# Layer norm of the first tile alone at the front: rstd by ACT, no bias operation, two warm matmuls fewer

## The chip, the cores and the metric

The kernel runs on one core of a Trainium2 chip. The metric is the device time of one execution in microseconds (us). PE is TensorE, DVE VectorE, ACT ScalarE, POOL GpSimd; SP issues the DMAs. PEclk is the granted clock of PE as a share of full speed. All runs below gave correct results, and all count as "fast" by the state rule; the differences are under 1%, so most kernels were timed five or six times, beside runs of the kernel before on the same chip.

## The reference

Four residual blocks over x of 2048 tokens by 512 features, in bf16: attention, feed-forward, attention, feed-forward, each behind a layer norm.

```
x = x + A(layernorm(x), wqkv, wo)     # linear attention, 32 heads of 16
x = x + B(layernorm(x), w1, w2)       # relu feed-forward, 1376 hidden
... the same two again
layernorm(x) = (x - mean(x)) / sqrt(var(x) + 1e-5)
A: q, k, v = x @ wqkv;  phi(t) = where(t > 0, t + 1, exp(t)) + 1e-6
   o = phi(q) (phi(k)^T v) / (phi(q) . sum phi(k));  A = o @ wo
```

## The kernel before

The 2048 tokens are 16 tiles of 128. The kernel is a list of operations with the buffers that they read and write; a list scheduler written in Python orders them for each engine, with a table of durations, a model of the DMA loads, and a seeded random search (1200 tries) that keeps an order when its modelled score, nearly the total time, is no worse. The order per engine is then fixed: an engine takes its instructions one by one, in program order, each behind waits on semaphores. This is why a small change of the operations gives another order of everything.

What matters here is the head, the first 25 us. The loads are issued in this order: x tile 0, x tiles 1-3, the K weights (wk), x tiles 4-7, the Q weights, more x. For tiles 0-3 each tile has its own layer norm and is transposed by PE; tiles 4-15 go in fours, and their transposes are DMAs of two tiles.

```
# cut: the layer norm of one of the tiles 0-3, before
if i in ACT_STATS:                       # tiles 2 and 3: sum and sum of squares by ACT
    ACT  activation(sqscr, xin[i], Identity, accum_out=s1)      # sm
    ACT  activation(sqscr, xin[i], Square,   accum_out=s2)      # sq
    DVE  mean, nm2, var                                          # three tiny operations
else:                                    # tiles 0 and 1
    DVE  bn_stats, bn_aggr
DVE  veps  = max(var, 0) + eps
POOL rstd  = veps ** -0.5
DVE  nbias = -mean * rstd
DVE or ACT  xn = xin * rstd + nbias      # norm
PE   4 transposes 128x128 into PSUM ; ACT or DVE copies them to Tb ; PE projects k (kproj)
# cut: warm-up, before any data is there
for k in range(12):  PE matmul of zeros, 128x512
# cut: the scheduler's model of a load: done = max(start + 1600, dma_free) + xfer_ns + 500
# cut: the choice in the scheduler: among operations that can start within 150 ns (DVE) of the
#      earliest one, the one of highest priority; priority of tile i is raised by 3000 * (16 - i)
```

## Time and profile before

Three runs at first, median 289.81 us (289.64 to 290.19); in later rounds single executions lie between 289.3 and 290.7, medians between 289.9 and 290.0.

The first part of the page, kernel before: busy time of each engine, its share of the span and its number of instructions.

```profile
PE 282.3 (98%) x1447; PEld 127.9 (44%) x1447; DVE 175.3 (61%) x482; ACT 177.7 (62%) x362; POOL 35.0 (12%) x45
```

PE is busy nearly all the time, but this counts 4.9 us of warm matmuls that compute nothing. The waits of PE, kernel before (who waited for whom, total, times, longest):

```profile
PE ps L563 <- DVE wrm L556: 1.2, 1, 1.2
PE ps L672 <- ACT Tb L642: 0.9, 2, 0.7
PE ps L672 <- DVE big L852: 0.5, 1, 0.5
PE ps L638 <- DVE xn L614: 0.4, 1, 0.4
PE ps L672 <- DMA Tb<-xn: 0.2, 1, 0.2
```

Only the wait on `big L852` (near 131 us) lies outside the head. The timeline of the head, kernel before, cut to the norms and to PE (start, duration, engine, line, operation, then in brackets the idle time ahead and what ended it):

```profile
3.69 0.18 DVE L583 BATCH_NORM_AGGREGATE mv<-bst 128x2 f32<-128x6 f32 x1
...
4.15 0.58 POOL L925 TENSOR_TENSOR rstd<-veps,nhalf 128x1 f32<-128x1 f32 x1 [1.72 <-DVE veps L923]
...
5.03 0.41 DVE L614 TENSOR_SCALAR xn<-xin,rstd,nbias 128x512 bf16<-128x512 bf16 x1
...
6.70 0.41 DVE L614 TENSOR_SCALAR xn<-xin,rstd,nbias 128x512 bf16<-128x512 bf16 x1
...
7.03 1.04 PE L672 MATMUL ps<-wqkv,Tb 128*128 128x512 bf16 x4 [0.69 <-ACT Tb L642]
...
8.52 1.29 DVE L582 BATCH_NORM_STATS2 bst<-xin 128x6 f32<-128x512 bf16 x2 [0.56 <-DMA xin<-in_A_x_dram]
...
8.98 1.04 PE L672 MATMUL ps<-wqkv,Tb 128*128 128x512 bf16 x4 [0.24 <-ACT Tb L642]
```

Tile 0's norm starts 1.16 us after its aggregate ended (3.87). The k projections of tiles 0 and 1 (kproj0, kproj1) start at 7.03 and 8.98. The chain that ended last, kernel before, in order of time (start, duration, what):

```profile
2.23 6.26 DMA xin<-in_A_x_dram
...
8.52 1.29 DVE bst L582 x2
...
19.60 5.17 DMA Tb<-xn
...
24.82 105.58 PE ps L672 x572
```

The chain does not run through PE's head, but through the load of x tiles 4-7, DVE, and the DMA transpose of tiles 8-9, which is used by kproj8 at 24.82. Two paths, PE's and DVE's, reach that point almost together.

### The profile page before, as it was taken

Reading aid. Unit: us, or ns where it says so; the run is one execution under the profiler, and the core shown is the slowest. Engines: PE = TensorE matmul, PEld = TensorE weight load, DVE = VectorE, ACT = ScalarE, POOL = GpSimd, SP = SyncE. Lnnn points to the kernel's source line nnn. Section 1 sums busy time; section 2 is a strip of 40 time slices with the busy share of each in tenths; the row PEclk is TensorE's granted clock in tenths of the full one; section 3 lists DMA queues with packets and bytes.
Section 4 is the critical chain, followed back from the end, with each engine's and each line's share of the span. In section 5 each row is a group of like instructions: output and inputs, shape, how many; then the busy total and the mean of one; then the engine's idle time right before and its main releaser. Section 6 shows DMA issues by size and latency. Waiting matters only on the chain.

```text
span 288.4 us, 3983 instructions
## 1 busy us (share of the span) xinstructions
PE 282.3 (98%) x1447; PEld 127.9 (44%) x1447; DVE 175.3 (61%) x482; ACT 177.7 (62%) x362; POOL 35.0 (12%) x45
## 2 busy tenths in 40 slices
PE   7999999999999999999999999999999999999996
PEld 2444454444444444443444444444444444444444
DVE  5899539998358652493345786899854954130233
ACT  5997649999666483586533665999966427316000
POOL 4211000002001110050301373000110011000000
PEclk9999999999999999999999999999999999999999
DMA  7976760213003070030003120012300323001022
GB/s 225 349 101 93 218 211 0 54 22 73 0 2 73 0 146 2 1 73 0 3 0 73 34 41 0 0 35 40 75 2 0 73 71 77 0 32 43 0 73 73
DMA packets 40163, 17.22 MB, mean 60 GB/s; under 512 B 31985, under 2 KB 39633, under 8 KB 40145
## 3 DMA queue, kind: packets, MB, share of 16 engines
q1 hardware_dynamic: 40144, 16.98, 24.8%
q8 instruction: 11, 0.18, 0.3%
q14 instruction: 8, 0.06, 0.1%
HBM read 7.01 MB, written 2.10 MB: 32 GB/s over the span
## 4 chain that ended last, share of the span: by engine, by line
PE 90%; DVE 4%; DMA 4%; SPq 0%; issue 0%; ACT 0%
PE ps L672 90%; DMA xin<-in_A_x_dram 2%; DMA Tb<-xn 2%; DVE bst L582 2%; DVE xn L614 1%; DVE big L658 0%; DVE emscr L656 0%; DVE big L852 0%; DVE mv L583 0%; ACT big L851 0%; DVE xin L870 0%; SPq L539 0%; SPq L534 0%; SPq L536 0%; DVE veps L590 0%
## 5 line engine op out<-in xcount | busy, mean ns | idle before, releaser
L672 PE MATMUL ps<-Tb,w 128*128 128x512 bf16 (+1 forms) x352 | 78.5, 379 | 0.5 <-DVE big L852 0.5
L672 PE MATMUL ps<-w,big 128*128 128x512 bf16 (+2 forms) x363 | 77.3, 372 | 0.0
L851 ACT ACTIVATE big<-ps 128x512 bf16<-128x512 f32 (+1 forms) x79 | 47.0, 601 | 28.2 <-PE ps L672 27.8
L679 ACT ACTIVATE sqscr<-xres 128x512 bf16<-128x512 f32 x48 | 30.0, 626 | 39.3 <-DVE xres L716 25.9
L672 PEld LDWEIGHTS ps<-w,big 128*128 128x128 bf16 (+1 forms) x363 | 35.5, 98 | 40.8
L672 PEld LDWEIGHTS ps<-Tb,w 128*128 128x128 bf16 (+1 forms) x352 | 34.5, 100 | 41.6 <-issue 1.8
L654 ACT ACTIVATE escr<-ps 128x512 bf16<-128x512 f32 x64 | 37.8, 617 | 8.4 <-PE ps L672 8.2
L652 ACT ACTIVATE big<-ps 128x512 bf16<-128x512 f32 x64 | 38.5, 619 | 2.5 <-PE ps L672 2.5
L712 DVE SCALAR_TENSOR_TENSOR xin<-ps,rstdf,xres 128x512 bf16<-128x512 f32 x15 | 11.3, 750 | 37.6 <-PE ps L672 37.5
L672 PE MATMUL ps<-wqkv,Tb 128*128 128x512 bf16 x128 | 31.9, 379 | 1.2 <-ACT Tb L642 0.9
L672 PE MATMUL ps<-big,xn 128*128 128x512 bf16 x128 | 32.2, 379 | 0.0
L658 DVE TENSOR_TENSOR big<-big,emscr 128x512 bf16<-128x512 bf16 x64 | 30.0, 484 | 3.4 <-ACT big L652 2.1
L656 DVE TENSOR_SCALAR emscr<-escr 128x512 bf16<-128x512 bf16 x64 | 21.2, 342 | 14.6 <-ACT escr L654 14.0
L672 PE MATMUL ps<-Tb,wqkv 128*128 128x512 bf16 x128 | 30.0, 379 | 0.0
L672 PE MATMUL ps<-Wp,big 128*128 128x512 bf16 x128 | 29.3, 379 | 0.0
L716 DVE SCALAR_TENSOR_TENSOR xres<-ps,rstdf,xres 128x512 f32<-128x512 f32 x16 | 12.0, 750 | 22.3 <-PE ps L672 22.1
L705 POOL TENSOR_TENSOR rstdf<-varf,nhalf 128x4 f32<-128x4 f32 x8 | 8.3, 1042 | 132.7 <-DVE nm2f L699 75.2
L830 DVE TENSOR_TENSOR big<-big,ps 128x512 bf16<-128x512 bf16 x32 | 20.0, 681 | 3.4 <-PE ps L672 3.4
L672 PEld LDWEIGHTS ps<-wqkv,Tb 128*128 128x128 bf16 x128 | 12.1, 98 | 16.2 <-ACT Tb L642 1.6
L672 PEld LDWEIGHTS ps<-Wp,big 128*128 128x128 bf16 x128 | 12.2, 98 | 15.4 <-DVE Wp L762 0.8
L672 PEld LDWEIGHTS ps<-Tb,wqkv 128*128 128x128 bf16 x128 | 12.2, 98 | 15.0 <-DVE nmf L688 0.5
L672 PEld LDWEIGHTS ps<-big,xn 128*128 128x128 bf16 x128 | 12.2, 98 | 14.6 <-issue 0.5
(89 smaller groups left out, 201.4 us busy)
## 6 DMA issues: line engine op xcount, KB each, us to landing
wqkv<-in_A_wqkv_dram SPq DMA_DIRECT2D x3, 512.0 KB, 7.2
xin<-in_A_x_dram SPq DMA_DIRECT2D x3, 512.0 KB, 8.2
out_dram<-xin SPq DMA_DIRECT2D x3, 512.0 KB, 2.9
w<-in_B_w_dram SPq DMA_DIRECT2D x1, 1376.0 KB, 6.5
w<-in_B_w_dram SPq DMA_DIRECT2D x1, 1280.0 KB, 9.6
wo<-in_A_wo_dram SPq DMA_DIRECT2D x1, 512.0 KB, 8.8
Tb<-xn SPq DMA_TRANSPOSE x30, 3.2
xin<-in_A_x_dram SPq DMA_DIRECT2D x1, 384.0 KB, 3.0
```

Of the source, the lines that this page charges most:

```text
L582: g.add(DVE, lambda e: e.bn_stats(bst[:, i, :], xin[:, i, :]), [("xin", i)], [("bst", i)], C_DVE_BNST, name="bnst%d" % i)
L652: g.add(ACT, lambda e: e.activation(dst_ap, psv[:, b, :], ACTF.Identity, bias=1.0 + 1e-6, scale=1.0), [("ps", b)], [dst_key], C_ACT_PSUM, ...
L654: g.add(ACT, lambda e: e.activation(escr[:, s, :], psv[:, b, :], ACTF.Exp), [("ps", b)], [("escr", s)], C_ACT_EXP, name=name + "_exp")
L656: g.add(DVE, lambda e: e.tensor_scalar(emscr[:, s, :], escr[:, s, :], 1.0, 1e-6, ALU.min, ALU.add), [("escr", s)], [("emscr", s)], C_DVE_B ...
L658: g.add(DVE, lambda e: e.tensor_tensor(dst_ap, dst_ap, emscr[:, s, :], ALU.max), [dst_key, ("emscr", s)], [dst_key], 340.0, name=name + "_ ...
L672: last = e.matmul(o, l, r, start=st, stop=sp, skip_group_check=skip)
L679: g.add(ACT, lambda e: e.activation(sqscr[:, q, :], xres[:, i, :], ACTF.Square, accum_out=dst[:, i:i + 1]), [("xres", i)], [("sqscr", q), ...
L705: g.add(POOL, lambda e: e.tensor_tensor(rstdf[:, sl], varf[:, sl], nhalf[:, 0:4], ALU.pow), [("varf", t), ("nhalf",)], [("rstdf", t)], C_P ...
L712: g.add(DVE, lambda e: e.scalar_tensor_tensor(xin[:, i, :], psv[:, b, :], rstdf[:, i:i + 1], xres[:, i, :], ALU.mult, ALU.add), rd, [("xin ...
L716: g.add(DVE, lambda e: e.scalar_tensor_tensor(xres[:, i, :], psv[:, b, :], rstdf[:, i:i + 1], xres[:, i, :], ALU.mult, ALU.add, accum_out= ...
L830: g.add(DVE, lambda e, j=j: e.tensor_tensor(unit_ap(us[j]), unit_ap(us[j]), psv[:, GB[j], :], ALU.mult), [("big", us[j]), ("ps", GB[j])], ...
L851: g.add_flex([(ACT, lambda e, M=M, b=b, u=u: e.activation(unit_ap(u, M), psv[0:M, b, :], ACTF.Relu), C_ACT_PSUM), (DVE, lambda e, M=M, b=b ...
```

## The change

Its intent: get tile 0 to PE sooner, by giving it the front of DVE and ACT, taking its rstd on ACT as exp(-0.5 ln(var + eps)) instead of over DVE, POOL and DVE, and folding the bias into the norm (subtract mean, multiply by rstd). PE's warm-up is shortened to match. Core of the diff (cut: the helper constants, and an option REM_TOK that stays off):

```diff
-WARM=12 ... SEARCH=1200 ... ACT_STATS=(2, 3)
+WARM=10 ... SEARCH=1500 ... ACT_STATS=(2,), RSTD_ACT=(0, 1), FILL=(0,), HEAD_DEP=True
 # tile 2, sum on ACT: now behind rstd of tile 0 (its Square is not)
-      [("xin", i)], [("sqscr", 0), ("s1", i)], C_ACT_SQ, name="sm%d" % i)
+      [("xin", i), ("rstd1", 0)], [("sqscr", 0), ("s1", i)], C_ACT_SQ, name="sm%d" % i)
 # tile 1, bn_stats: now behind the norm of tile 0 (tile 3's is not)
-      ln_stats_first(i)
+      ln_stats_first(i, [("xn", i - 1)] if 0 < i < 3 and HEAD_DEP else [])
+if i in RSTD_ACT:                                        # tiles 0 and 1
+      ACT lnv  = Ln(var + eps)
+      ACT rstd = Exp(-0.5 * lnv)
+else:                                                    # tiles 2 and 3 keep veps and POOL
-DVE nbias = -mean * rstd
-ln_norm(i, True, keys=[("rstd1", i), ("nbias1", i)])     # ACT or DVE
+DVE xn = (xin - mean) * rstd
 # behind the transposes of tile 0
+PE one matmul of zeros, 128x512                          # the filler
```

More of the change, by code (lines that the diff above doesn't have):

```diff
@@ L24 @@
 C_ACT_SQ = 620.0
+C_ACT_TINY = 220.0
 C_DVE_PSUM = 600.0
@@ L406, in build_kernel @@
 def build_kernel(nc, A_x, A_wqkv, A_wo, B_w1, B_w2, out, n_layers_pairs=2, Q_LATE=3, O_PE_CHUNKS=3, PHI_PATH=3,
-                 KV_LAG=2, INTERLEAVE=True, WARM=12, SPLIT_CHUNKS=1, TAIL_SPLIT=True,
+                 KV_LAG=2, INTERLEAVE=True, WARM=10, SPLIT_CHUNKS=1, TAIL_SPLIT=True,
                  PHI_K=3, PHI_QE=3, PHI_QL=3, LAST_HALVES=True, ZH_FIRST=True, P2_TIGHT=False,
-                 FIRST_PE_CHUNKS=1, TGK=2, TGF=2, FT_PE=0, WP_GB=True, WO_LAG=1, DEN_PRE=1, LATE_A=1, ITERS=12, BOOST=3000.0, SEARCH=1200, ZP=(0, 3), WK_ACT=False, ACT_STATS=(2, 3)):
+                 FIRST_PE_CHUNKS=1, TGK=2, TGF=2, FT_PE=0, WP_GB=True, WO_LAG=1, DEN_PRE=1, LATE_A=1, ITERS=12, BOOST=3000.0, SEARCH=1500, ZP=(0, 3), WK_ACT=False, ACT_STATS=(2,), REM_TOK=False, RSTD_ACT=(0, 1), FILL=(0,), HEAD_DEP=True):
     S = A_x.shape[1]
@@ L474, in build_kernel @@
         zhl = sb("zhl", [128, 2, 512], BF16)
+        hrt = sb("hrt", [128, 2, 4, 128], BF16)
+        eps5 = sb("eps5", [128, 1], F32)
+        lnv = sb("lnv", [128, NT], F32)
         GT = sb("GT", [128, 4, 512], BF16)
@@ L501, in build_kernel @@
         psv = _PS()
-        scr_state = {"e": 0, "sq": 0, "ln": 0}
+        scr_state = {"e": 0, "sq": 0, "ln": 0, "rem": 0}
         def dma(emit, reads, writes, xfer_ns, name, eng=SP, issue=C_SP_ISSUE):
@@ L568, in build_kernel @@
         g.add(POOL, lambda e: e.memset(eps6[:], 1e-6), [], [("eps6",)], 100, name="ms_eps6")
+        g.add(POOL, lambda e: e.memset(eps5[:], EPS), [], [("eps5",)], 100, name="ms_eps5")
         g.add(POOL, lambda e: e.memset(ones[:], 1.0), [], [("ones",)], 200, name="ms_onesb")
@@ L579, in build_kernel, with ln_stats_first @@
               [("m1f",)], [("bmask",)], 300, name="as3")
-        def ln_stats_first(i):
-            g.add(DVE, lambda e: e.bn_stats(bst[:, i, :], xin[:, i, :]), [("xin", i)], [("bst", i)], C_DVE_BNST, name="bnst%d" % i)
+        if REM_TOK:
+            g.add(POOL, lambda e: e.memset(hrt[:], 0.0), [], [("hrt0",), ("hrt", 0), ("hrt", 1)], 400, name="ms_hrt")
+        def ln_stats_first(i, behind=()):
+            g.add(DVE, lambda e: e.bn_stats(bst[:, i, :], xin[:, i, :]), [("xin", i)] + list(behind), [("bst", i)], C_DVE_BNST, name="bnst%d" % i)
             g.add(DVE, lambda e: e.bn_aggr(mv[:, i, :], bst[:, i, :]), [("bst", i)], [("mean", i), ("var", i)], C_DVE_SMALL, name="bnag%d" % i)
@@ L605, in ln_chunk, with ln_norm @@
                   [("mean", i) for i in tl] + [("rstd", t)], [("nbias", t)], C_DVE_SMALL, name="nbias%d" % t)
-        def ln_norm(i, first, eng=None, keys=None):
+        def ln_norm(i, first, eng=None):
             t = i // 4
@@ L610, in ln_norm @@
             skey = ("xin", i) if first else ("xres", i)
-            rd = [skey] + (keys or [("rstd", t), ("nbias", t)])
+            rd = [skey, ("rstd", t), ("nbias", t)]
             alts = [(ACT, lambda e: e.activation(xn[:, i, :], src, ACTF.Identity, scale=rstd[:, i:i + 1], bias=nbias[:, i:i + 1]),
@@ L627, in tr_chunk, with transpose_pe @@
                 tr_dma(lo, lo + grain)
-        def transpose_pe(i):
+        def transpose_pe(i, fill=False):
             b = alloc_bank()
@@ L639, in _emit @@
                 return last
-            g.add(PE, _emit, [("xn", i), ("ident",)], [("ps", b)], 4 * C_MM128, name="trp%d" % i)
+            g.add(PE, _emit, [("xn", i), ("ident",)], [("ps", b)] + ([("fill", i)] if fill else []), 4 * C_MM128, name="trp%d" % i)
+            if fill:
+                g.add(PE, lambda e: e.matmul(psv[:, wt, :], wrm[:, 0:128], wrm[:, :], start=True, stop=True),
+                      [("fill", i)], [("ps", wt)], C_MM512, name="fill%d" % i)
             dst = Tb[:, i, :, :].rearrange("p c t -> p (c t)")
@@ L841, in build_kernel, with b_h_rem, src @@
         hcount = [0]
+        def b_h_rem(t, c, M, b):
+            r = scr_state["rem"]
+            scr_state["rem"] = (r + 1) % 2
+            mm_group(lambda: [(psv[:, b, M * il:M * il + M], Tb[:, 4 * t + il, d, :], w1[:, d, 128 * c:128 * c + M],
+                               d == 0, d == 3, False) for il in range(4) for d in range(4)],
+                     [("T", i) for i in range(4 * t, 4 * t + 4)] + [("w1",)], [("ps", b)], 16 * (M / 2.4 + 2.5), "hr%d" % t)
+            def src():
+                return psv[:, b, 0:4 * M].rearrange("p (i m) -> p i m", m=M)
+            g.add_flex([(ACT, lambda e: e.activation(hrt[:, r, :, 0:M], src(), ACTF.Relu), C_ACT_PSUM - 80.0),
+                        (DVE, lambda e: e.tensor_scalar(hrt[:, r, :, 0:M], src(), 0.0, None, ALU.max), C_DVE_FLEX - 120.0)],
+                       [("ps", b), ("hrt0",)], [("hrt", r)], name="hrr%d" % t)
+            u = h_unit(c, t)
+            dma(lambda e: e.dma_start_transpose(unit_ap(u).rearrange("p (i t) -> p i t", t=128),
+                                                hrt[:, r, :, :].rearrange("p i m -> p (i m)")),
+                [("hrt", r)], [("big", u)], 2200.0, "hrt%d" % t, issue=C_SP_TR)
         def b_h(t):
-            for c in range(NFC):
+            for c in ([NFC - 1] + list(range(NFC - 1)) if REM_TOK else range(NFC)):
                 M = 128 if c < NFC - 1 else FLAST
                 b = alloc_bank()
+                if REM_TOK and M < 128:
+                    b_h_rem(t, c, M, b)
+                    continue
                 mm_group(lambda b=b, c=c, M=M: [(psv[0:M, b, :], w1[:, d, 128 * c:128 * c + M], Tb[:, 4 * t:4 * t + 4, d, :],
@@ L921, in ln_tile_first @@
             else:
-                ln_stats_first(i)
-            g.add(DVE, lambda e: e.tensor_scalar(veps[:, c], mv[:, i, 1:2], 0.0, EPS, ALU.max, ALU.add),
-                  [("var", i)], [("veps1", i)], C_DVE_SMALL, name="veps%d" % i)
-            g.add(POOL, lambda e: e.tensor_tensor(rstd[:, c], veps[:, c], nhalf[:, 0:1], ALU.pow),
-                  [("veps1", i), ("nhalf",)], [("rstd1", i)], C_POOL_POW1, name="rstd%d" % i)
-            g.add(DVE, lambda e: e.scalar_tensor_tensor(nbias[:, c], mv[:, i, 0:1], -1.0, rstd[:, c], ALU.mult, ALU.mult),
-                  [("mean", i), ("rstd1", i)], [("nbias1", i)], C_DVE_SMALL, name="nbias%d" % i)
-            ln_norm(i, True, keys=[("rstd1", i), ("nbias1", i)])
+                ln_stats_first(i, [("xn", i - 1)] if 0 < i < 3 and HEAD_DEP else [])
+            if i in RSTD_ACT:
+                g.add(ACT, lambda e: e.activation(lnv[:, c], mv[:, i, 1:2], ACTF.Ln, bias=eps5[:, 0:1]),
+                      [("var", i), ("eps5",)], [("lnv", i)], C_ACT_TINY, name="lnv%d" % i)
+                g.add(ACT, lambda e: e.activation(rstd[:, c], lnv[:, c], ACTF.Exp, scale=-0.5),
+                      [("lnv", i)], [("rstd1", i)], C_ACT_TINY, name="rstd%d" % i)
+            else:
+                g.add(DVE, lambda e: e.tensor_scalar(veps[:, c], mv[:, i, 1:2], 0.0, EPS, ALU.max, ALU.add),
+                      [("var", i)], [("veps1", i)], C_DVE_SMALL, name="veps%d" % i)
+                g.add(POOL, lambda e: e.tensor_tensor(rstd[:, c], veps[:, c], nhalf[:, 0:1], ALU.pow),
+                      [("veps1", i), ("nhalf",)], [("rstd1", i)], C_POOL_POW1, name="rstd%d" % i)
+            g.add(DVE, lambda e: e.tensor_scalar(xn[:, i, :], xin[:, i, :], mv[:, i, 0:1], rstd[:, c], ALU.subtract, ALU.mult),
+                  [("xin", i), ("mean", i), ("rstd1", i)], [("xn", i)], C_DVE_NORM_BF, name="norm%d" % i)
         def ln_first(t):
@@ L936, in ln_first @@
                     if t < FIRST_PE_CHUNKS:
-                        transpose_pe(i)
+                        transpose_pe(i, i in FILL)
                     for o in g.ops[n0:]:
```

## The prediction

> **What bounds the kernel now.** The page gives PE 282.3 of 288.4 us busy (98%). The waits view gives PE 3.2 us of waits: 1.2 before the first warm matmul, 0.9 on the ACT copy of transposed tiles, 0.4 on a DVE norm, 0.5 on a DVE relu near 131 us, 0.2 on a DMA transpose. So only the head can give anything; 4.9 us of its busy time are the 12 warm matmuls. The chain view runs there not through PE: the DMA of x tiles 4-7 lands at 8.50, DVE follows almost without pause to 19.60, the DMA transpose of tiles 8-9 to 24.77; then PE to the end.
>
> **Head before (timeline).** x0 lands 2.97; bn_stats to 3.66, bn_aggr, veps, POOL pow 4.15-4.73, nbias 4.85, norm0 5.03-5.44: 1.16 us from the end of the aggregate (3.87) to the norm. Transposes start at 5.96, right behind the last warm matmul (start 5.74); PE took matmuls 0.43 us apart until about 5.5, then about 0.22, as the Trainium skill ("TensorE: Matmul & The Clock Gate", Part 1) states for a cold and a warm array. ACT copy 6.38, kproj0 7.03, kproj1 8.98, kproj2 about 10.7.
>
> **What changes.** Tiles 0 and 1: veps, POOL and nbias go; ACT Ln and Exp come. By the skill ("ScalarE: Activation LUTs", What ACT_TABLE_LOAD costs) one column costs about 0.19-0.28 us each. With hand-overs I estimate 0.65 us from aggregate to norm: norm0 at about 4.5-4.9. Ten warm matmuls end at about 5.5 (estimate), so they, not the norm, now gate the transposes: copy at about 5.9, kproj0 at about 6.55 (wk lands at 6.00). Gain at kproj0: 0.45 us. Tile 1's statistics now wait for norm0, but no POOL, no nbias: norm1 about 6.5, kproj1 about 7.9 (before 8.98). Tile 3's statistics move from ACT (about 1.6 us) to DVE (0.69); kproj2 about 8.8 against 10.7. The filler costs 0.22 us in a gap: nothing. PE could thus be 1 to 1.7 us ahead by kproj3.
>
> **How much survives.** Not all. x tiles 4-7 still land at 8.50; from there to 24 DVE is full. DVE loses after 8.50 only nbias3 and norm3 (0.55 us), and ACT's freed 1 us may take over a norm. The transpose of tiles 4-5 landed 0.2 us before use, that of tiles 8-9 at the moment of use (kproj8, 24.82). So PE, running ahead, will wait for these. Tiles 10-15 had 2.6 us of slack. I expect 0.5 to 1.2 us to survive at 25 us. After that PE is gapless and the rest carries the gain unchanged, except that the list schedule's random search now runs over other operations: plus or minus 0.3 us.
>
> **Prediction: 288.9 us, 80% range 288.3 to 289.7.** Faster by over 2%: 0.01; within 2%: 0.98; slower by over 2%: 0.01.
>
> **What the profile would show.** PE busy about 281.5; Ln and Exp of 128x1 on ACT, 0.2-0.28 us each, no second table load; norm0 about 4.5; transposes behind the tenth warm matmul at about 5.5; kproj0 about 6.5, kproj1 under 8.2; kproj8 at 23.6-24.3, new or longer PE waits on DMA transposes between 15 and 25; POOL pow 128x1 only twice.
>
> **What would make it wrong.** The clock rising later with less warm-up, so that first projections run cold; ACT being busy with tile 2's statistics when Ln, Exp or the copies are due; the new schedule gaining more by moving norms to ACT (down to 288) or opening waits elsewhere (no gain).

## The result

The changed kernel: 290.63 us median of six (290.07 to 291.92), against 289.91 us for the kernel before. The ratio is 1.003, 95% interval 1.0009 to 1.0051 (a ratio is the mean time of one kernel's runs over that of the other's of the same rounds, so not quite the ratio of the medians). It is slower by 0.7 us, where 0.9 us faster had been predicted. One of the six executions, the 291.92, had a granted clock of 0.994, the others 1.000. All outputs are right.

The first part of the page, changed kernel:

```profile
PE 282.0 (98%) x1446; PEld 127.8 (44%) x1446; DVE 175.6 (61%) x476; ACT 177.2 (61%) x361; POOL 34.0 (12%) x44
```

Busy times are as good as unchanged, so the difference lies in waits. The waits of PE, changed kernel:

```profile
PE ps L646 <- DVE xn L964: 2.1, 2, 1.6
PE ps L567 <- DVE wrm L560: 1.2, 1, 1.2
PE ps L683 <- ACT Tb L653: 0.5, 1, 0.5
PE ps L683 <- DVE Tb L654: 0.2, 1, 0.2
```

The waits for the DMA transpose and near 131 us are gone. A new one, of 1.6 us, is for a norm. The timeline of the head, changed kernel (columns as before):

```profile
3.93 0.29 ACT L955 ACTIVATE lnv<-mv,eps 128x1 f32<-128x1 f32 x1 [1.87 <-DVE mv L591]
4.47 0.63 ACT L944 ACTIVATE sqscr<-xin 128x512 bf16<-128x512 bf16 x1 [0.25 <-DMA xin<-in_A_x_dram]
4.47 0.69 DVE L590 BATCH_NORM_STATS2 bst<-xin 128x6 f32<-128x512 bf16 x1 [0.58 <-DMA xin<-in_A_x_dram]
...
5.10 0.18 ACT L957 ACTIVATE rstd<-lnv 128x1 f32<-128x1 f32 x1
...
5.49 0.40 DVE L964 TENSOR_SCALAR xn<-xin,mv,rstd 128x512 bf16<-128x512 bf16 x1
...
7.04 1.04 PE L683 MATMUL ps<-wqkv,Tb 128*128 128x512 bf16 x4 [0.47 <-ACT Tb L653]
...
7.32 0.20 ACT L957 ACTIVATE rstd<-lnv 128x1 f32<-128x1 f32 x1
...
8.87 0.69 DVE L590 BATCH_NORM_STATS2 bst<-xin 128x6 f32<-128x512 bf16 x1 [1.35 <-DMA xin<-in_A_x_dram]
9.48 0.72 DVE L964 TENSOR_SCALAR xn<-xin,mv,rstd 128x512 bf16<-128x512 bf16 x2
9.93 0.72 PE L646 MATMUL ps<-ident,xn 128*128 128x128 bf16 x8 [1.64 <-DVE xn L964]
...
10.85 2.76 PE L683 MATMUL ps<-wqkv,Tb 128*128 128x512 bf16 x12 [0.20 <-DVE Tb L654]
...
25.68 1.03 PE L683 MATMUL ps<-wqkv,Tb 128*128 128x512 bf16 x4
```

Two things are out of order; which tile a line belongs to follows from the program order that the kernel's scheduler made.

1. At the front. On ACT the Square of tile 2 (4.47) stands between tile 0's Ln (3.93) and Exp (5.10), and it waits for x tiles 1-3. On DVE the bn_stats of tile 3 (4.47) is ahead of norm 0. So norm 0 starts at 5.49, later than before (5.03), and kproj0 at 7.04, as before (7.03). The new dependencies had been put on tile 2's sum and tile 1's statistics; its Square and tile 3's statistics took the places.
2. Farther on. The rstd of tile 1 is ready at 7.52. But on DVE the bn_stats of tile 4 comes first, and that waits for its data until 8.84. Norms 1 and 2 start at 9.48. PE waits 1.64 us, and kproj1 starts at 10.85 instead of 8.98.

The Trainium skill ("TensorE: Matmul & The Clock Gate", Architectural detail) says that ACT and DVE queues are strictly first in, first out; the trace agrees: norm 1 stood ready for almost 2 us behind an instruction that was waiting for a DMA.

The chain that ended last, changed kernel:

```profile
2.23 6.61 DMA xin<-in_A_x_dram
...
8.87 0.69 DVE bst L590
9.56 0.33 DVE xn L964
...
10.85 121.24 PE ps L683 x644
```

It now runs over that bn_stats and norm into PE. kproj8 starts at 25.68 instead of 24.82: 0.86 us lost in the head. (In these two executions x tiles 4-7 landed at 8.84 and at 8.50, so up to 0.34 us of this may be the load and not the order.) From kproj8 to the start of the last DVE operation it is 260.39 us (286.07 - 25.68), against 260.88 before (285.70 - 24.82): 0.49 us won later, about the size of the wait near 131 us. The two spans thus differ by only 0.3 us; the medians differ by more, because the execution of before that was profiled (290.33) is a slow one of its spread.

### The profile page after: what moved, and what is told of

It reads as the page before. It is cut to its first block, busy times and chain, and to the rows that moved or that the text cites. A ratio compares the mean times of both kernels' runs of the same rounds, so it can differ in the third digit from the quotient of the medians.

```text
span 288.7 us, 3973 instructions
## 1 busy us (share of the span) xinstructions
PE 282.0 (98%) x1446; PEld 127.8 (44%) x1446; DVE 175.6 (61%) x476; ACT 177.2 (61%) x361; POOL 34.0 (12%) x44
## 3 DMA queue, kind: packets, MB, share of 16 engines
HBM read 7.01 MB, written 2.10 MB: 32 GB/s over the span
## 4 chain that ended last, share of the span: by engine, by line
PE 95%; DMA 2%; DVE 1%; SPq 0%; issue 0%
PE ps L683 95%; DMA xin<-in_A_x_dram 2%; DVE bst L590 0%; DVE xin L901 0%; SPq L543 0%; DVE Tb L654 0%; SPq L538 0%; PE ps L646 0%; SPq L540 0%; DVE xn L964 0%
## 5 line engine op out<-in xcount | busy, mean ns | idle before, releaser
L882 ACT ACTIVATE big<-ps 128x512 bf16<-128x512 f32 (+1 forms) x78 | 46.4, 600 | 27.8 <-PE ps L683 27.4
```

Source lines behind the costliest of these rows:

```text
L882: g.add_flex([(ACT, lambda e, M=M, b=b, u=u: e.activation(unit_ap(u, M), psv[0:M, b, :], ACTF.Relu), C_ACT_PSUM), (DVE, lambda e, M=M, b=b ...
```

## The experiments

Theory A: the program order in the head made the loss; norms 1 and 2 stand behind a bn_stats whose data comes late. Its root would be the scheduler's model of the loads, in which x tiles 4-7 land at 6.97 and norm 1 can start at 7.40; the model's clock starts about 0.75 us after the trace's, so the model has 7.7 where the traces have 7.91 to 9.27. Rival B: the head does not matter, and the search, or DVE's path to tiles 8-9, decides. A small helper, `behind(engine, names, after)`, moves operations within one engine's finished program order and derives the waits anew; all else stays as it is.

### e1_stats4_behind_norms: one move

```diff
+behind(DVE, ["bnst4"], "trev3")    # was: bnst4, norm1, norm2, trev1, trev3
```

> The changed kernel with one move in DVE's program order: the bn_stats of tile 4 goes from ahead of norm 1, norm 2 and the two DVE copies of transposed tiles to behind them; everything else is in the same order. Theory A (DVE, which works in program order, stands at the bn_stats of tile 4 until the load of x tiles 4-7 lands at 8.84, while norm 1 was ready at about 7.6): PE's longest wait in the head, 1.6 us, goes to under 0.4; kproj1 starts at about 9.0 instead of 10.85, kproj8 at 24.3 to 24.9 instead of 25.68, time 0.8 to 1.3 us below the changed kernel, so 289.3 to 289.9, at or a little below the kernel before. Rival B (the head does not matter; the longer time comes from the reseeded schedule later in the kernel, or from the DVE and DMA path of tiles 4-9): kproj1 may come earlier, but kproj8 stays within 0.2 us of 25.68 and the time does not move.

Measured: 289.74 us (289.56 to 289.99), 0.9 us below the changed kernel; ratio to before 0.9992 (0.9978 to 1.0006). Norms 1 and 2 and tile 4's bn_stats in its timeline of DVE:

```profile
7.42 0.41 DVE L964 TENSOR_SCALAR xn<-xin,mv,rstd 128x512 bf16<-128x512 bf16 x1
8.04 0.41 DVE L964 TENSOR_SCALAR xn<-xin,mv,rstd 128x512 bf16<-128x512 bf16 x1 [0.20 <-POOL rstd L962]
...
9.22 0.68 DVE L590 BATCH_NORM_STATS2 bst<-xin 128x6 f32<-128x512 bf16 x1
```

The norms no longer wait for the load. Its timeline of PE, kproj1 and kproj4:

```profile
9.03 2.76 PE L683 MATMUL ps<-wqkv,Tb 128*128 128x512 bf16 x12
...
17.81 1.04 PE L683 MATMUL ps<-wqkv,Tb 128*128 128x512 bf16 x4 [0.49 <-DMA Tb<-xn]
```

Norm 1 starts at 7.42, kproj1 at 9.03, kproj8 at 24.73. As theory A said; rival B falls. A piece of B stays true: kproj1 is 1.82 us earlier, kproj8 only 0.95. In between, PE's waits view has 0.4 us for a DVE operation of tiles 4-7 (nbias, at 13.91) and 0.5 us for the DMA transpose of tiles 4-5; part of the gain ends there. The longest wait was therefore 0.5 us, not under 0.4 as expected.

### e2_exp_first: only the front

```diff
+behind(ACT, ["sq2"], "rstd0")                       # Exp of tile 0 before Square of tile 2
+behind(DVE, ["bnst3", "bnag3", "veps3"], "norm0")
```

> The changed kernel with only the front put as its title says: on ACT the Square of tile 2 goes behind the Exp of tile 0, on DVE the statistics of tile 3 go behind norm 0. Theory A2: norm 0 starts at about 4.6 instead of 5.49, the first transposes at about 5.5 (behind the tenth warm matmul) instead of 5.95, kproj0 at about 6.5 instead of 7.04. Because tile 4's bn_stats still stands in front of norms 1 and 2, kproj1 and kproj8 stay where they were (10.85 and 25.68, each within 0.3) and the time stays within 0.3 us of the changed kernel. If the late norm 0 were what makes the kernel slow, kproj8 and the time would come about 0.5 us earlier.

Measured: norm 0 at 4.48 and kproj0 at 6.32 in the profiled execution, as intended, 0.7 us earlier than in the changed kernel. The time is 291.29 us (290.04 to 292.59). Three executions had a clock of 1.000 or 0.999 and took 290.04 to 290.68, like the changed kernel at full clock (290.07 to 290.97), so for these the expectation holds; three had 0.994 and took 291.91 to 292.59. The median is higher because three of six fell in the low clock instead of one of six; so few executions don't show that e2 falls more often. The profiled one is of the low ones. Its timeline of PE, from the transposes of tile 3 to the projections of tiles 1 to 3:

```profile
7.20 0.40 PE L646 MATMUL ps<-ident,xn 128*128 128x128 bf16 x4
10.36 0.72 PE L646 MATMUL ps<-ident,xn 128*128 128x128 bf16 x8 [2.77 <-DVE xn L964]
11.28 4.45 PE L683 MATMUL ps<-wqkv,Tb 128*128 128x512 bf16 x12 [0.19 <-DVE Tb L654]
```

In the same execution, busy time and clock in two stretches (columns: stretch, its length, busy time and count of PE, PEld, DVE, ACT, POOL, then PEclk, DMA share, GB/s):

```profile
7.60:10.30 2.70, 0.00 (x0) 0.00 (x0) 1.00 (x3) 0.88 (x2) 0.44 (x1) 1.00 1.05 357
11.20:15.60 4.40, 4.32 (x13) 1.66 (x14) 4.33 (x17) 2.37 (x5) 1.01 (x1) 0.61 0.83 263
```

PE waited 2.77 us; then its clock was 0.61 in the mean, and twelve projection matmuls took 4.45 us instead of 2.76: 1.7 us more. In finer stretches the clock was 0.50 from about 11.4 to 14.8, so it fell about 1 us after PE had begun again. The Trainium skill ("TensorE: Matmul & The Clock Gate", Part 1, and the table in Why this matters for your kernels) says that the clock falls to half after a window of about 3.4 us without enough work, and advises against gaps over about 3 us. The trace agrees in kind. The gap is 1.13 us longer than in the changed kernel's trace: PE was through with tile 3's transposes 0.7 us earlier, while tile 1 still stood behind tile 4's bn_stats, and the load was 0.4 us later (DVE took up tile 4 at 9.30). The expectation of "no change" had no place for this cost. The one execution of the changed kernel at 0.994 has the same mark; it was not profiled.

### e3_both_moves

Both edits together.

> Both moves together. Theory A: kproj0 at about 6.5, kproj1 at about 9.0; kproj8 and the time as with the first move alone, within 0.3 us, since kproj1 is held by norms 1 and 2 and not by kproj0. If the moves add up, it is 0.5 us faster than the first alone (about 289.0).

Measured: 289.52 us (289.47 to 289.56); ratio to before 0.9984 (0.9970 to 0.9997). kproj1 at 8.83, a wait of 0.52 us on the DMA transpose of tiles 4-5 at 17.63. So 0.2 us faster than e1: the moves do not add up, and the order farther on was the costly one. The two moves together turn the loss of 0.7 us into a gain of 0.5, on the same operations.

### b1_norm3_first: the same idea in the kernel before

```diff
+behind(DVE, ["bnst6", "bnst4"], "norm3")   # was: bnst6, bnst4, nbias3, norm3
```

> The kernel before with one move: nbias 3 and norm 3 on DVE go ahead of the bn_stats of tiles 6 and 4, behind which they stood ready (POOL had rstd 3 at about 8.6, norm 3 began at 9.90). If PE's path through the head is what bounds it, PE's wait of 0.36 us before the transposes of tile 3 goes and kproj8 (24.82) and the time come 0.3 us earlier. If DVE and the DMA transpose of tiles 8-9, which landed 0.05 us before kproj8, bound it as well, as I think, kproj2 comes about 0.4 us earlier, kproj8 stays within 0.15 us of 24.82 and the time within 0.2 us of the kernel before.

Measured: 290.74 us (290.11 to 291.13), ratio 1.0022 (1.0007 to 1.0038): slower, where equal was expected. Its waits for DMA transposes, from the PE timeline (the first is new, the second was 0.24 us before):

```profile
18.09 1.04 PE L672 MATMUL ps<-wqkv,Tb 128*128 128x512 bf16 x4 [0.19 <-DMA Tb<-xn]
...
25.54 1.04 PE L672 MATMUL ps<-wqkv,Tb 128*128 128x512 bf16 x3 [0.38 <-DMA Tb<-xn]
```

PE's wait for norm 3 is gone, and the kernel is slower all the same: "norms first" is no rule. A likely reading is that DVE's path to the DMA transposes bounds the head of the kernel before, and that this path pays for the statistics of tiles 4 and 6 being held back. The trace does not show it: in this execution x tiles 4-7 landed at 9.11, 0.61 us later than in the trace of before, and the transposes of tiles 8-9 landed 0.73 us later (25.50 against 24.77), most of which the load explains. The clock also rose later (the twelve warm matmuls took 5.30 us instead of 4.88), but so it did in the trace of b3, which has the same head as before and one of its faster times (289.59), with kproj8 at 24.52. How the 0.8 us divide stays open.

### e4_load_model and b2_load_model: the root

```diff
-    1600.0 * (4 - lo) / 4.0, "ld_x%d" % t)
+    1600.0 * (4 - lo) / 4.0 + (900.0 if t == 1 else 0.0), "ld_x%d" % t)
```

In e4 this is the only edit to the changed kernel, in b2 to the kernel before; the search runs again.

> The changed kernel with one number of its own scheduler corrected: the model of the DMA loads lets x tiles 4-7 land 0.9 us later (7.87 instead of 6.97 on the model's clock, which starts about 0.75 us after the trace's; the trace has 8.36 to 9.27). The schedule is searched again, with the same seed. Theory A, root cause: the program order of DVE was wrong because the scheduler believed that tile 4's data is there before norm 1 is ready. The new order has norm 1, norm 2 and a copy ahead of the first bn_stats of tiles 4-7, so the head wait behind that bn_stats goes: PE's longest wait between 7 and 12 us under 0.5, kproj1 at about 9.0, no execution with a granted clock under 0.999, time 289.2 to 289.9. Rival: the time is set by the luck of the search; then it lies anywhere from 289.3 to 291.

> The kernel before with the same correction of the load model, searched again: the control for the run e4_load_model. Before already had norms 0 to 2 ahead of tile 4's statistics, so the correction has little to repair: within 0.5 us of before either way (289.5 to 290.5), by the luck of the search. If it gains as much as the changed kernel does (about 1 us), the correction is good for any kernel and says nothing of the change.

Measured: e4 288.86 us (288.58 to 289.02), ratio to before 0.9958 (0.9945 to 0.9972): 1.8 us below the changed kernel and 1.1 below before. b2 290.66 us, ratio 1.0019 (1.0004 to 1.0035): the correction by itself gains nothing there, it even loses about 0.5 us. Both times lie outside what was expected, e4 by 0.3 us on the fast side, b2 by 0.2 us on the slow side. The timeline of DVE in e4, norms, a copy, then tiles 4-7:

```profile
7.02 1.36 DVE L964 TENSOR_SCALAR xn<-xin,mv,rstd 128x512 bf16<-128x512 bf16 x3
8.61 0.42 DVE L654 COPY Tb<-ps 128x512 bf16<-128x512 bf16 x1 [0.23 <-PE ps L646]
8.95 1.87 DVE L590 BATCH_NORM_STATS2 bst<-xin 128x6 f32<-128x512 bf16 x3
```

The three norms now run ahead of tile 4-7's statistics, and none of them stands ready for long. From the chain that ended last, e4:

```profile
9.09 121.10 PE ps L683 x644
```

From kproj1 on PE works without a gap until near 130 us. Looking only at the orders that the scheduler builds, with eight seeds each: in the changed kernel norms 1 and 2 are behind a bn_stats of tiles 4-7 eight times out of eight, with the corrected load no norm is, eight times out of eight. (Seeds 1 to 8 give this; a ninth, 11, has norm 2 alone behind a bn_stats in the changed kernel.) So the order is hardly an accident of the search.

### e6_after_seed3 and e7_load_model_seed3: luck of the search

```diff
-    rng = random.Random(7)
+    rng = random.Random(3)
```

e6 is the changed kernel, e7 is e4, both with this seed.

> The changed kernel with its search seeded with 3 instead of 7 and nothing else. Its scheduler gives this one 284.72 us on its own model, 0.59 less than the changed kernel (285.31) and 0.12 more than the run e4_load_model (284.60), but norms 1 and 2 stand behind the statistics of tiles 4-7 on DVE, as they do for all eight seeds looked at. Theory A (the order in the head decides, and the model is blind to it): the head wait of 1.5 us or more is there again, kproj1 after 10.3, and the time is 289.7 to 290.7, at least 0.7 above e4_load_model. Rival (luck of the search decides): the time follows the model, so about 289.0.

> The run e4_load_model with seed 3: the worst of eight seeds on the corrected model (285.43 us, 0.83 above e4_load_model and 0.13 above the changed kernel), with no norm of tiles 0-3 behind the statistics. Theory A: no long wait in the head, kproj1 at about 9, no execution under clock 0.999; slower than e4_load_model by what the search lost later, 289.2 to 289.8, but faster than the changed kernel by at least 0.8. Rival (luck of the search): 290.4 or more.

Measured: e6 290.89 us (290.23 to 292.50), two of six executions under clock 1, PE's longest wait 2.1 us for a norm. Its modelled total was the best of the eight seeds of the changed kernel, its time among the worst (0.2 us above what was expected): the model is blind to this loss. e7 290.01 us (289.40 to 290.62), no low clock, kproj1 at 9.09. With seed 3 the corrected load is worth 0.88 us (290.89 to 290.01), with seed 7 1.77 us (290.63 to 288.86). The expectation for e7 missed by 0.2 us, and e7 is 0.6 us below the changed kernel with seed 7 instead of at least 0.8: 1.15 us between e4 and e7 is what one seed or another is worth, of which its trace shows 0.6 us as a PE wait at 17 us. So the order of the norms is the cause of the loss, but the size of e4's gain over before is in part the luck of its search.

### e5_exp_first_fillers: the clock

```diff
 # e2, and behind the transposes of tile 3:
+for _ in range(14):
+    e.matmul(psv[:, b, 256:512], wrm[:, 0:128], wrm[:, 0:256], start=True, stop=True)
```

> The run e2_exp_first, with 14 matmuls of 256 columns on zeros behind the transposes of tile 3 (1.5 us of PE work in its 2.8 us wait, into the unused half of a PSUM bank, result unused). Three of six executions of e2_exp_first had a granted clock of 0.994 and took 291.9 to 292.6; the other three 290.0 to 290.7. Theory C: a long PE wait in the head makes the clock gate fall back for one window in some executions (12 projections took 4.45 us instead of 2.76), about 1.7 us lost each time. Then with the fillers no execution is under 0.999 and all lie at 290.0 to 290.8, median about 290.4. Rival: the slow executions come from a late load of x; then about half stay at 292, fillers or not.

Measured: 290.12 us (289.83 to 291.08), no execution under 0.999, its median 1.2 us below that of e2 by useless work alone. None of six against three of six would be thin by itself. But six of the 18 executions of the changed kernel, e2 and e6, the kernels whose profile has a PE wait of 1.6 us or more, were under 0.999, and not one of the 68 executions of the other runs or of 44 of the kernel before. So the fall of the clock behind a long wait accounts for e2's slow half. Why only some executions fall stays open; in the two traces with a fall (e2, e6) the ten warm matmuls took 3.96 and 4.08 us, against 4.24 to 4.45 in the other traces with ten, that is, the clock had risen earlier. One execution of e5 at 291.08 with full clock is not explained.

### b3_relu_first: the gain far from the head

```diff
+behind(DVE, ["q0_2_phi"], "hrelu3_0")   # kernel before, near 131 us
```

> The kernel before with one move far from the head: on DVE, near 131 us, the relu of the first hidden block of chunk 3 goes ahead of the phi operation of the last but one query group, as it stands in the changed kernel. Theory D: the new search gave the changed kernel about 0.5 us there (PE's wait of 0.54 us on that relu is gone from its trace), which hides part of the loss in the head. Then this run is 0.4 to 0.55 us faster than before, about 289.5, and PE's wait near 131 us is gone. Otherwise it is within 0.2 us of before.

Measured: 289.63 us against 289.92, ratio 0.9989 (0.9974 to 1.0005). The wait near 131 us is gone from its trace. The sign is as expected, the size 0.3 instead of 0.4 to 0.55, and the interval does not exclude zero: plausible, not shown.

### e10_no_tile0_first: which part put norm 1 there

```diff
-... ACT_STATS=(2,), RSTD_ACT=(0, 1), FILL=(0,), HEAD_DEP=True
+... ACT_STATS=(2,), RSTD_ACT=(0, 1), FILL=(0,), HEAD_DEP=False
-      [("xin", i), ("rstd1", 0)], [("sqscr", 0), ("s1", i)]
+      [("xin", i)], [("sqscr", 0), ("s1", i)]
```

> The changed kernel without its two new dependencies (tile 1's bn_stats behind norm 0, tile 2's sums behind rstd 0), everything else of the change kept: Ln and Exp for the rstd of tiles 0 and 1, no nbias, ten warm matmuls, the filler, the uncorrected load model; searched again with seed 7. In its order norm 1 is ahead of the statistics of tiles 4-7, norm 2 still behind the first of them, but PE wants tile 2 only after kproj1. Theory A says that what hurt is norm 1 behind tile 4's bn_stats, and the order built says that the dependency of tile 1 on norm 0 put it there: then kproj1 starts at about 8.7, no execution is under clock 0.999, and the time is 289.0 to 289.9, at least 0.7 below the changed kernel. If the rest of the change is to blame, it stays at 290.4 or more.

Measured: 289.36 us (289.08 to 289.65), 1.3 us below the changed kernel; ratio to before 0.9982 (0.9969 to 0.9995); no low clock. Norm 1 starts at 6.42 and PE at tile 1 at 8.40:

```profile
8.40 1.03 PE L683 MATMUL ps<-wqkv,Tb 128*128 128x512 bf16 x4
```

Norm 0 is then at 5.77, later than in the changed kernel, and this kernel is faster than both all the same. So the very part named in the title, tile 0 alone at the front, is what hurt: holding tile 1 for tile 0 brought norm 1 so late that, in the model, tile 4's data was there first (tile 4's bn_stats can start at 7.01, norm 1 at 7.40). The search ran again here, so its luck is in the number; but with each of four seeds looked at, the order without these dependencies has norm 1 ahead of the statistics of tiles 4-7.

### e8_best_exp_first, e9_twelve_warm, e11_best_no_filler: the best version and the small parts

e8 is e4 with the front as intended; e9 is e4 with two more warm matmuls in the same order; e11 is e8 with the filler cut to one column.

```diff
 # e8
+behind(ACT, ["sq2"], "rstd0");  behind(DVE, ["bnst3", "bnag3", "veps3"], "bnst1")
 # e9
-for k in range(WARM):
+for k in range(WARM + 2):
 # e11, the filler
-matmul(psv[:, wt, :],   wrm[:, 0:128], wrm[:, :])
+matmul(psv[:, wt, 0:1], wrm[:, 0:128], wrm[:, 0:1])
```

> The run e4_load_model with the two moves at the front: Square of tile 2 behind Exp of tile 0 on ACT, the statistics of tile 3 behind those of tile 1 on DVE. norm 0 at about 4.5 instead of 5.4, kproj0 at about 6.6 instead of 7.09, kproj1 at about 8.7 instead of 9.09. From there the DMA transpose of tiles 4-5 is the next bound: it landed 0.08 us before its use in e4_load_model, and depends on x tiles 4-7, not on tile 0. So I expect a new PE wait of 0.2 to 0.4 us on it at about 17.6 and a gain of only 0 to 0.2 us: 288.6 to 288.9. If it is 0.4 faster, the front is worth what it gains at kproj1.

> The run e4_load_model with twelve warm matmuls emitted instead of ten, in the same schedule. In e4_load_model the tenth warm matmul had ended when norm 0 was ready (transposes at 5.79). Two more end at about 5.95 to 6.35, as the clock's rise falls, so the transposes and kproj0 come 0.2 to 0.5 us later and kproj1 0 to 0.4 later: the time 0.1 to 0.4 us longer (289.0 to 289.3). If warm matmuls do not matter because kproj1 waits for norms 1 and 2 anyway, it is within 0.1.

> The run e8_best_exp_first with the filler behind the first transposes cut from 512 columns to one, in the same order. The filler ran at 5.54 to 5.92 in a stretch in which PE waited for the copy anyway, so without it kproj0 is at 6.4 as before. If it keeps the clock up, some executions now show cold first projections or a granted clock under 0.999 and the time is 0.2 us or more longer; I expect within 0.1 us: 288.6 to 288.8.

Measured: e8 288.67 us (288.63 to 288.72), ratio to before 0.9951 (0.9940 to 0.9963): better than both kernels, and its five executions lie within 0.1 us. Its front:

```profile
3.90 0.29 ACT L955 ACTIVATE lnv<-mv,eps 128x1 f32<-128x1 f32 x1 [1.83 <-DVE mv L591]
4.23 0.20 ACT L957 ACTIVATE rstd<-lnv 128x1 f32<-128x1 f32 x1
4.40 0.63 ACT L944 ACTIVATE sqscr<-xin 128x512 bf16<-128x512 bf16 x1
4.46 0.41 DVE L964 TENSOR_SCALAR xn<-xin,mv,rstd 128x512 bf16<-128x512 bf16 x1 [0.60 <-ACT rstd L957]
...
6.39 1.04 PE L683 MATMUL ps<-wqkv,Tb 128*128 128x512 bf16 x4 [0.47 <-ACT Tb L653]
```

From the aggregate's end (3.86) to norm 0 it is 0.60 us instead of 1.16. kproj0 comes 0.7 us earlier than in e4, kproj1 only 0.08 (9.01), the time 0.2: tile 0 is not the bound. The wait on the DMA transpose that I had expected did not show. e9: 289.18 us (288.90 to 289.28), ratio to before 0.9968 against 0.9958 for e4, so about 0.3 us slower; kproj0 at 7.27, kproj1 at 9.27. The intervals of the two ratios overlap, so the size is not certain; the sign is as expected. The trace does not show the expected way, though: its transposes waited 0.30 us for norm 0, not for the warm matmuls, because x tiles 1-3 landed at 4.68 instead of 4.29 in e4. So what two warm matmuls cost is not shown. e11: 288.60 us (288.56 to 288.65), no low clock: the filler does nothing that these runs could see.

## Why the prediction was wrong

- **PE bounds, and only the head can give anything: right for the most part.** Where one move repaired the order of the head, kproj1, kproj8 and the time came earlier together (e1). But 0.49 us was won behind kproj8, about the size of the wait near 131 us that the prediction listed and did not count.
- **0.65 us from aggregate to norm 0, norm 0 at 4.5: right as a cost, not for this kernel.** With Exp next to Ln it was 0.60 us and 4.46 to 4.48 (e2, e8). In the changed kernel it was 5.49, because Square 2 and the statistics of tile 3 got in. "ACT being busy with tile 2's statistics" stood among the risks. Alone it was not what cost the time.
- **"norm1 about 6.5, kproj1 about 7.9": the step that failed.** Measured 9.48 and 10.85, so 2.95 us late at kproj1. I added up durations in the order in which I wished them to run. But the order is made by the scheduler, and DVE takes it literally. The sum lacked the term "wait of tile 4's bn_stats for x tiles 4-7", 1.35 us of DVE idle and then 0.6 us of its run. Before's trace showed the landing (8.50) and the two bn_stats that waited for it; I used them only for tiles 4-7 and not as something that could stand in front of tile 1. The other 1 us is norm 0's: it came at 5.49 instead of 4.5, tile 1's statistics wait for it, and so tile 1's rstd was ready only at 7.52. With norm 0 in time (4.43 in e3, 4.46 in e8) the statistics of tile 3 stood among those of tile 1 on DVE, and that rstd was still not ready before 7.3. Repairing the order took away the 1.95 us only: in e1, e3, e4 and e8 kproj1 came at 8.83 to 9.09, at most 0.15 us earlier than before (8.98). The 1.1 us predicted at kproj1 showed in none of them; without the hold on tile 1 (e10) it was 0.6 (8.40).
- **"PE could be 1 to 1.7 us ahead by kproj3": wrong in sign for this kernel.** PE began the group behind the last projection of tiles 0-3 at 13.45; before, at 12.33. With the order repaired (e8) it was 11.61, 0.7 us ahead.
- **"0.5 to 1.2 us survive": not tested by the changed kernel; the repaired orders had 0.5 (e3), 1.1 (e4) and 1.4 (e8) against before.** The first has the changed kernel's own order elsewhere; the other two have another search.
- **PE waits on DMA transposes between 15 and 25 us: true in some repaired orders** (0.49 us in e1, 0.52 in e3), not in e4 and e8, and absent in the changed kernel, where PE came too late to wait.
- **"Plus or minus 0.3 us" for the new search: too small.** The stretch behind kproj8 won 0.49; two seeds of the same kernel differed by 1.15 (e4, e7).
- **"The clock rising later": it rose in time; it fell again.** It did so in one of six executions of the changed kernel and three of six of e2; e2's trace shows 1.7 us lost, behind a long wait. I had not thought of a fall.
- **The filler costs nothing: right** (e11).

Open: how much of e4's and e8's lead over before is the search and how much the change; why single executions of the kernel before differ by up to 1.4 us at full clock (the landing of x tiles 4-7 and the moment at which the clock rises differ among the traces, but each trace is one execution); how b1's loss divides; why the clock falls in some executions and not in others.

## What to carry to other kernels

An engine that works in program order waits for its next instruction, not for its most urgent one: before costing a change by durations, write down the new order on each engine, and look there for an instruction that waits for a DMA ahead of work that PE needs. If a scheduler makes the order, compare its modelled landing of each load with the trace, since a wrong time turns into a wrong order, and its own total doesn't show it; compare several seeds before a half per cent is put down to a change. A gain at the first tile is worth nothing if the second is held for it, and a PE gap of 2 to 3 us can cost its clock on top.

## What the Trainium skill lacked or had wrong

- "TensorE: Matmul & The Clock Gate", table in Why this matters for your kernels: it advises against PE gaps over about 3 us. Here the clock fell in executions whose longest PE wait in the profile was 2.77 us (e2, with only transposes between projections that lay 3.9 us apart) and 2.1 us (e6, projections 2.6 us apart, clock 0.53 in the mean from 11.6 to 15.2 us), and not in every execution: three of six, two of six, and one of six of the changed kernel, whose profiled wait was 1.6. No run tried a wait between 0.7 and 1.6 us; where the longest in the profile, past the one ahead of the warm-up, was 0.7 us or less, no clock under 0.999 was seen.
- "ScalarE: Activation LUTs", What ACT_TABLE_LOAD costs: the figures hold for one column (0.29 us for Ln with a pointer bias, 0.18 to 0.20 for Exp). What it doesn't give is the way across engines: from the aggregate's end on DVE over Ln and Exp to the start of the norm took 0.60 us, of which the two records cover 0.49.
- "DMA: Bandwidth & Descriptors": I found no figure there for how much the landing of one load in a queue of loads differs from execution to execution. x tiles 4-7, the fourth load, landed between 7.91 and 9.27 us in the traces of these 16 kernels, though all issue the same four loads first.
